# Strassen cross network: two 1024-row lanes that share each weight load, a second Strassen level in W22*T4, and two residual adds moved to DMA

## The chip, the cores and the metric

One core of a Trainium2 chip runs the kernel. The metric is the device time of one execution in microseconds (us), the median of several executions. Engines: PE is the matmul engine (PEld its weight load), DVE the vector engine, ACT the scalar engine, POOL is GpSimd, SP the engine that here only issues DMAs.

## The reference, cut to what matters

```python
B, Din, L = 16384, 1024, 6                  # bf16
def reference(x0, ws, bs):
    x = x0
    for l in range(L):
        proj = jnp.einsum('bd,de->be', x, ws[l]) + bs[l]
        x = x0 * proj + x
    return x
```

Rows are independent, so the kernel takes 1024 rows through all six layers and then takes the next 1024. x lives transposed (features on partitions), so x0 is transposed when it is loaded and the result is transposed again before it is stored. Both transposes are done by DMA.

## The kernel before: the parts that matter

Each layer is a 2x2 block product done with seven products in place of eight (Strassen, in Winograd's form). The product with W21 is itself done with seven half-size products, a second level. Weight combinations are built during the first pair of 512-row halves and saved to DRAM (`Lc`). Later pairs load eight 0.5 MB weight tiles per layer, up to eleven ahead.

```python
x0t_pool = ctx.enter_context(tc.tile_pool(name="x0t", bufs=2))   # x0 of this pair and of the next
xst_pool = ctx.enter_context(tc.tile_pool(name="xst", bufs=2))   # x of this pair and of the one before
wring    = ctx.enter_context(tc.tile_pool(name="wring", bufs=14))
PREF = 11
# ...
def tt(out, in0, in1, op):                                       # every DVE add, subtract, multiply
    nc.vector.tensor_tensor(out=out, in0=in0, in1=in1, op=op)
# ...
for pr in range(NPAIR):                     # 16 pairs of 512 + 512 rows
    for l in range(L):                      # 24 groups of four 128x512 matmuls
        # ...                               # and 7 small products of four 128x256 matmuls
        if l == (2 if pr == 0 else 0) and not last_pair:         # x0 of the NEXT pair, early
            x0T_next = x0t_pool.tile([P, 2, KD, NB], BF16, name="x0T")
            for n in range(2):
                tr = nc.sync.dma_start_transpose(out=x0T_next[:, n], in_=x0[...])
    # ... after the last layer: the result is transposed into the OLD x0 tile, then stored
    nc.sync.dma_start_transpose(out=xo, in_=xst[:].rearrange("r n k b -> r (n k b)"))
    for n in range(2):
        nc.sync.dma_start(out[...], x0T[:, n]...)
```

## Time and profile before

| | before |
|---|---|
| median | 2343.75 us (3 runs, 2342.72 to 2345.05) |
| PE, DVE, ACT busy | 97%, 86%, 78% |
| one layer of one pair, from the timeline | 23.78 us |
| 96 layers at 23.80 us | 2285 us |
| the rest of the profiled span of 2342.7 us: start, first pair's boundaries, end | 58 us |

Two lines of the page of the kernel before: busy us of each engine (share of the span) x instructions, and the shares of the chain of work that ended last.

```profile
PE 2277.5 (97%) x11668; PEld 1164.1 (50%) x11904; DVE 2003.2 (86%) x2160; ACT 1818.9 (78%) x2977; POOL 1.1 (0%) x5
...
PE 87%; DVE 10%; issue 1%; ACT 1%; SPq 1%; DMA 0%; DVEq 0%
```

PE sets the pace. What a matmul costs is read from the timeline, from start to start, because the second column (the duration) overlaps the next instruction. These are five lines of the timeline of the kernel before.

```profile
2276.54 1.03 PE L233 MATMUL pA_88<-xst,wp 128*128 128x512 bf16 x4
2277.41 1.03 PE L233 MATMUL pA_89<-xst,wp 128*128 128x512 bf16 x4
...
2286.90 0.60 PE L245 MATMUL pX_92<-xst,wp 128*128 128x256 bf16 x4
2287.34 0.60 PE L245 MATMUL pX_93<-ti,wp 128*128 128x256 bf16 x4
...
2300.32 1.03 PE L233 MATMUL pA_88<-xst,wp 128*128 128x512 bf16 x4
```

A group of four wide matmuls takes about 0.865 us, one of four narrow ones 0.44 us. From 2276.54 to 2300.32, one layer, it is 23.78 us.

The change from one pair to the next: these are the DMA queue of SP in the timeline, and the windows view of the same stretch (window and its length; busy us of PE, PEld, DVE, ACT, POOL; granted clock; DMA share of the 16 engines; GB/s), kernel before.

```profile
1191.49 9.73 SPq L374 DMA_TRANSPOSE x0T<-xst  x1
1201.32 0.52 SPq L83 DMA_DIRECT2D wp<-in_ws_dram  x1
...
1203.12 5.79 SPq L377 DMA_DIRECT2D out_dram<-x0T  x2
...
1215.50 10.67 SPq L355 DMA_TRANSPOSE x0T<-in_x_dram  x2
```

### The profile page before, as it was taken

What the parts mean: (1) busy time and instruction counts of PE and PEld (TensorE: products, weight loads), DVE (VectorE), ACT (ScalarE), POOL (GpSimd) and SP (SyncE); (2) the same over time, 40 slices, a digit from 0 to 9 for tenths busy, and PEclk for the clock granted to TensorE, in tenths of its full rate; (3) what the DMA queues carried; (4) which work ended last, traced back from release to release, by engine and by line L of the source; (5) the groups of instructions that cost most, each with busy time, mean ns of one, the idle gap of its engine ahead of it and who ended that gap; (6) DMA issues with size and microseconds to landing.
All of it is one profiled execution on the core that took longest, in us unless ns stands there. A gap on an engine that the chain in (4) does not pass through costs nothing.

```text
span 2342.7 us, 31963 instructions
## 1 busy us (share of the span) xinstructions
PE 2277.5 (97%) x11668; PEld 1164.1 (50%) x11904; DVE 2003.2 (86%) x2160; ACT 1818.9 (78%) x2977; POOL 1.1 (0%) x5
## 2 busy tenths in 40 slices
PE   6989999999999999999999999999999999999996
PEld 2445555555454555555555545454555555554543
DVE  5998888888889788888888888888898888988886
ACT  4767777878787787778787878778777777787775
POOL 0000000000000000000000000000000000000000
PEclk8999999999999999999999999999999999999998
DMA  7659669595785958759586695967859578595853
GB/s 242 198 198 239 229 193 267 182 257 198 206 256 185 274 187 213 252 178 284 174 222 240 189 276 171 254 206 207 253 189 271 193 204 257 175 284 178 234 191 81
DMA packets 613837, 508.60 MB, mean 217 GB/s; under 512 B 399664, under 2 KB 552240, under 8 KB 613680
## 3 DMA queue, kind: packets, MB, share of 16 engines
q1 hardware_dynamic: 613680, 506.53, 72.5%
q8 instruction: 95, 1.56, 0.3%
q14 instruction: 62, 0.51, 0.1%
HBM read 390.07 MB, written 49.28 MB: 188 GB/s over the span
## 4 chain that ended last, share of the span: by engine, by line
PE 87%; DVE 10%; issue 1%; ACT 1%; SPq 1%; DMA 0%; DVEq 0%
PE pA_91 L233 13%; PE pA_88 L233 13%; PE pA_89 L233 13%; PE pA_90 L233 12%; PE pX_92 L245 7%; PE pX_94 L233 6%; PE pX_93 L233 6%; PE pX_95 L233 6%; PE pX_92 L233 6%; DVE ev L91 4%; PE pX_93 L245 3%; DVE xst L91 2%; PE pX_94 L245 2%; DVE wp L91 1%; DVE ti L91 1%
## 5 line engine op out<-in xcount | busy, mean ns | idle before, releaser
L233 PEld LDWEIGHTS <-wp 128*128 128x128 bf16 x9216 | 901.4, 98 | 1026.5 <-issue 55.1
L91 DVE TENSOR_TENSOR ev<-ev,x0T 128x2048 bf16<-128x2048 bf16 x384 | 469.8, 1223 | 9.9
L91 DVE TENSOR_TENSOR xst<-ev,xst 128x2048 bf16<-128x2048 bf16 x320 | 384.9, 1224 | 21.7 <-DVE ev L91 0.5
L91 DVE TENSOR_TENSOR ev<-ev 128x2048 bf16<-128x2048 bf16 x288 | 352.2, 1223 | 38.0 <-ACT ev L249 25.7
L245 PEld LDWEIGHTS <-wp 128*128 128x128 bf16 x2688 | 262.7, 98 | 133.2
L252 ACT ACTIVATE ev<-pA_88,b_all 128x512 bf16<-128x512 f32 x288 | 198.4, 689 | 69.9 <-PE pA_88 L233 65.7
L252 ACT ACTIVATE ev<-pA_90,b_all 128x512 bf16<-128x512 f32 x288 | 198.1, 688 | 34.9 <-PE pA_90 L233 33.4
L252 ACT ACTIVATE ev<-pA_91,b_all 128x512 bf16<-128x512 f32 x288 | 197.9, 687 | 34.0 <-PE pA_91 L233 34.0
L252 ACT ACTIVATE ev<-pA_89,b_all 128x512 bf16<-128x512 f32 x288 | 198.3, 689 | 25.6 <-PE pA_89 L233 1.8
L245 PE MATMUL pX_92<-ti,wp 128*128 128x256 bf16 x1152 | 172.8, 273 | 1.1
L249 ACT CAST ev<-pX_92 128x512 bf16<-128x512 f32 x192 | 112.3, 585 | 28.8 <-PE pX_92 L233 16.7
L233 PE MATMUL pA_88<-xst,wp 128*128 128x512 bf16 x320 | 83.0, 382 | 22.4 <-DVE xst L91 22.4
L252 ACT ACTIVATE ev<-pX_92,b_all 128x512 bf16<-128x512 f32 x96 | 66.0, 687 | 26.6 <-PE pX_92 L233 24.3
L233 PE MATMUL pA_89<-xst,wp 128*128 128x512 bf16 x314 | 83.2, 385 | 0.3
L233 PE MATMUL pA_91<-xst,wp 128*128 128x512 bf16 x315 | 82.3, 381 | 0.6
L233 PE MATMUL pX_94<-xst,wp 128*128 128x512 bf16 x320 | 82.1, 379 | 0.3
L233 PE MATMUL pA_90<-xst,wp 128*128 128x512 bf16 x306 | 81.7, 385 | 0.4
L233 PE MATMUL pX_93<-xst,wp 128*128 128x512 bf16 x308 | 80.5, 379 | 0.7
L233 PE MATMUL pX_95<-xst,wp 128*128 128x512 bf16 x308 | 80.5, 379 | 0.3
L233 PE MATMUL pX_92<-xst,wp 128*128 128x512 bf16 x306 | 80.3, 379 | 0.4
L252 ACT ACTIVATE ev<-pX_93,b_all 128x512 bf16<-128x512 f32 x96 | 66.0, 687 | 16.9 <-PE pX_93 L233 15.7
L252 ACT ACTIVATE ev<-pX_94,b_all 128x512 bf16<-128x512 f32 x96 | 66.0, 687 | 16.9 <-PE pX_94 L233 16.9
(2831 smaller groups left out, 3586.4 us busy)
## 6 DMA issues: line engine op xcount, KB each, us to landing
wp<-Lc SPq DMA_DIRECT2D x450, 512.0 KB, 4.3
wp<-in_ws_dram SPq DMA_DIRECT2D x288, 512.0 KB, 4.9
out_dram<-x0T SPq DMA_DIRECT2D x30, 1024.0 KB, 10.2
Lc<-wp SPq DMA_DIRECT2D x30, 512.0 KB, 6.3
out_dram<-xoS SPq DMA_DIRECT2D x4, 512.0 KB, 4.7
w_98<-in_ws_dram SPq DMA_DIRECT2D x1, 512.0 KB, 5.0
x0T<-in_x_dram SPq DMA_TRANSPOSE x32, 7.3
w_151<-in_ws_dram SPq DMA_DIRECT2D x1, 512.0 KB, 5.4
```

The costliest lines, as they stand in the source:

```text
L91: nc.vector.tensor_tensor(out=out, in0=in0, in1=in1, op=op)
L233: nc.tensor.matmul(dst[m][:], lhsT=wt[:, k, m * P:(m + 1) * P], rhs=rhs[:, k, :], start=(start and k == 0), stop=(k == KH - 1), skip_group ...
L245: nc.tensor.matmul(dst[:, m * NQ:(m + 1) * NQ], lhsT=wv[:, k, m * P:(m + 1) * P], rhs=ti[i][:, k, :], start=(start and m == 0 and k == 0), ...
L249: nc.scalar.copy(out=dst, in_=src)
L252: nc.scalar.activation(out=dst, in_=src, func=IDENT, bias=bias_col(eh, m), scale=1.0)
```

## The change

The intent has three parts. (1) Two lanes of 1024 rows take turns layer by layer, so a weight tile is loaded once for both, and the dependent work of one lane (sums, differences, residual) runs under the matmuls of the other. (2) From the second lane pair on, the product W22*T4 also gets a second Strassen level: 20 groups and 14 small products per unit (one layer of one lane) instead of 24 and 7. (3) The residual adds of two of four quarters of x are done by an accumulating DMA from GpSimd's queue in layers 1 to 4. The memory for the second lane comes out of the double buffers.

The diff, cut to its core (helpers, first-pass weight combinations and the order of evictions left out):

```diff
-    x0t_pool = ctx.enter_context(tc.tile_pool(name="x0t", bufs=2))
-    xst_pool = ctx.enter_context(tc.tile_pool(name="xst", bufs=2))
-    wring = ctx.enter_context(tc.tile_pool(name="wring", bufs=14))
+    wring = ctx.enter_context(tc.tile_pool(name="wring", bufs=RING))        # RING = 10
+    x0L = [res.tile([P, 2, KD, NB], BF16, name=f"x0L{i}") for i in range(2)]   # one per lane
+    xL = [res.tile([P, 2, KD, NB], BF16, name=f"xL{i}") for i in range(2)]     # one per lane
# ...
+    def load_x0(lp, lane, eh, n):                      # a quarter, over the old x0, in place
+        r0 = lp * LB + lane * PR + n * NB
+        nc.sync.dma_start_transpose(out=q(x0L[lane], eh, n), in_=x0[r0:r0 + NB, eh * H:(eh + 1) * H])
+    def store_quarter(lp, lane, eh, n, xf):
+        # ...
+        nc.sync.dma_start_transpose(out=dst, in_=xf[:].rearrange("r j k p -> r (j k p)"))   # dst in xL
+        nc.sync.dma_start(out[r0:r0 + NB, eh * H:(eh + 1) * H]..., q(xL[lane], eh, n)...)
# ...
+    l2_of = lambda lp: (2,) if lp == 0 else (2, 4)     # products with a second level
+    units = [(lp, l, lane) for lp in range(NLP) for l in range(L) for lane in range(2)]
# ...
+        def x_out(c, eh, n):
+            if last_layer:
+                xf = late["xf"].tile([P, KH, KH, P], BF16, name="xf")          # pool of 2
+                tt(xf[:]..., c..., q(xst, eh, n)..., ADD)
+                store_quarter(lp, lane, eh, n, xf)
+            elif l > 0:
+                nc.gpsimd.dma_start(q(xst, eh, n), c, accum_op=ADD)
+            else:
+                tt(q(xst, eh, n), c, q(x0T, eh, n), ADD)
+        def finish(c, add, eh, n):
+            tt(c, c, add, ADD)
+            tt(c, c, q(x0T, eh, n), MULT)              # last use of this quarter of x0 ...
+            if nxt_x0:
+                load_x0(lp + 1, lane, eh, n)           # ... so it can be overwritten only now
+            x_out(c, eh, n)
```

A lane-pair switch, the term used below, is the passage from layer 5 of one lane pair to layer 0 of the next. There are seven, and each brings eight x0 loads and eight output transposes, every one a quarter of a lane (0.5 MB).

## The prediction

> What bounds the kernel now. The page gives PE 97% of 2342.7 us, DVE 86%, ACT 78%; the chain of waits is 87% PE, 10% DVE. In the timeline four 128x512 matmuls (one group) take 0.8645 us, four 128x256 ones 0.4365 us. One layer of a 1024-row pair is 24 groups plus 7 second-level products: 24 x 0.8645 + 7 x 0.4365 = 23.80 us, and the timeline shows 23.78 from layer to layer. 96 of these are 2285 us. The other 58 us are the start (first matmul at 11.8 us, then matmuls at half rate until 16.5), the first pair's layer boundaries where the new weights' combinations sit on DVE (the waits: PE for DVE's xst, 22.4 us in 5 times, each followed by slow matmuls), and 18 us after the last matmul.
>
> What the change does to PE. A layer of a lane becomes 20 groups plus 14 small products: 17.29 + 6.11 = 23.40 us, in 84 of 96 units (the first lane pair keeps 23.80). Sum 2251 us: 34 us less. All of it is critical.
>
> Boundaries. A lane's dependent work runs under the other lane, so the 22 us of boundary waits should go. The start gets worse: the second small product needs the combination of W21, W21 itself and the first differences; by the trace's durations PE stands until about 25 us (now 11.8). I put the start at 27 us lost, the tail at 19 as now. 2251 + 27 + 19 = 2297.
>
> DVE. A 128x512 add costs 0.42 us, a 128x2048 one 1.22; issued back to back 0.34 and 1.14. A wide 128x4096 one I estimate at 2.3. A middle layer then needs about 21.2 us of 23.4 (now 20.9 of 23.8); layers 0 and 5, without the DMA adds, about 23.6, thus just over PE. DVE goes to about 93% busy, with no slack in those layers. ACT drops a little: evictions of two banks at once.
>
> DMA. Weights are read 9 times 0.5 MB per two units instead of 16 times: queue share falls from 72% to about half. The new risk is the accumulating DMA. The Trainium skill (DMA: Bandwidth & Descriptors, Anatomy of one DMA) gives about 2 us fixed plus bytes/436 GB/s; with two reads per write, and traffic, my estimate is 6 to 9 us for 0.5 MB; no run here shows one yet. After the x12 product DVE does 8 us of other work before it needs the sum; the loop closes at landing time + 13.4 us per unit, so up to 10 us cost nothing, and each further us costs 1 us in 56 to 64 units. Descriptors come from GpSimd, beside a DVE always at two-input adds; SBUF — State Buffer (Who interferes with whom) says such adds take only the shared read port.
>
> Lane-pair switch. 16 quarter transposes at 2.4 us of SP issue each (DMA issues: 2.4 for xoS) plus stores that wait for them share the queue with weight loads only one ring ahead. I charge about 2 us of PE per switch, 15 us in all, and 6 us for small stalls.
>
> Predicted 2318 us, range 2283 to 2375. Chances: faster by over 2% 0.28, within 2% 0.57, slower 0.15.
>
> What would show it: middle layers at 23.4 us per lane in the timeline; no PE wait for DVE's xst in the first layers; PE first continuous at about 25 us; DVE over 90%; accumulating DMAs landing under 10 us; PE gaps, if any, at the switches, waiting for weights.
>
> What would make it wrong: accumulating DMAs over 10 us (then DVE stands before its first difference and PE follows: slower); the SP queue blocked in the switches for 8 us or more each (plus 60 us); or everything hidden (about 2290).

## More of the kernel before

```profile
1190.00:1200.00 10.00, 9.95 (x59) 5.67 (x58) 4.30 (x6) 7.72 (x14) 0.00 (x0) 1.00 0.99 211
1200.00:1210.00 10.00, 9.95 (x49) 4.73 (x49) 9.66 (x10) 8.46 (x14) 0.00 (x0) 1.00 1.08 266
1210.00:1220.00 10.00, 9.95 (x53) 5.12 (x53) 9.15 (x11) 7.82 (x14) 0.00 (x0) 1.00 1.06 219
```

For 30 us the DMA share is about 1, so the engines are busy all the time by this measure. (The share adds up the times of packets. It goes over 1, so packets overlap, and it does not tell how much room is left.) One output transpose and two x0 transposes keep SP for 20 us. PE nevertheless works 9.95 of each 10 us. Nothing that PE needs at that moment depends on those transfers.

## The result, and the profile after

The change made the kernel slower: 2417.51 us median (4 runs, 2416.68 to 2417.71) against 2344.4 us for the kernel before (4 runs). The ratio is 1.0311 (95% interval 1.0293 to 1.0329). Ratios here are the mean time of one kernel's runs over that of the other's of the same rounds, so not quite the ratio of the medians quoted. The time is above the predicted range, which ended at 2375.

The same two lines of the page, kernel after.

```profile
PE 2286.9 (95%) x12912; PEld 1269.5 (53%) x12912; DVE 2116.1 (88%) x2096; ACT 1783.9 (74%) x2485; POOL 110.7 (5%) x133
...
PE 77%; DVE 15%; DMA 5%; SPq 1%; issue 1%; ACT 1%; DVEq 0%; ACTq 0%
```

PE's share of the chain fell from 87% to 77%, and DMA appears with 5%. To see where, I took the time from one unit's first eviction on ACT to that of the next unit. This is worked out from the trace and is not a view of the profile. Rows are lane pairs; columns are the 12 units of one, layer by layer, lane 0 and lane 1.

```
before (two pairs per row)
2  23.8  23.8  23.8  23.8  23.8  23.8  23.8  23.8  23.8  23.8  23.8  23.8 | 285.3
after
0  33.5  23.8  24.0  23.8  23.8  23.8  23.8  23.8  23.8  23.8  23.8  23.8 | 295.3
1  35.9  24.9  24.1  23.4  23.4  23.4  23.4  23.4  23.4  23.4  23.4  23.4 | 295.3
2  37.5  25.0  24.1  23.4  23.4  23.4  23.4  23.4  23.4  23.4  23.4  23.4 | 297.0
...
6  38.6  24.3  24.1  23.4  23.4  23.4  23.4  23.4  23.4  23.4  23.4  23.4 | 297.5
```

Nearly everything went as counted. Middle units take 23.4 us, the first lane pair has no stalls between layers, and PE ends 18 us before the span does. Only the first unit or two of lane pairs 1 to 7 are long. Those seven rows sum to 2083.2 us, against 7 x 12 x 23.4 = 1965.6. The excess is 118 us, 17 us per switch, and without it the kernel would be at about 2299 us. By the trace, 86 us of the excess are gaps of PE (39 gaps of over 0.3 us), and about 32 us are matmuls at half clock after them (65 us of granted clock 0.5 in the switches).

What PE waits for, waits view of the kernel after (engine, line, waited for: us in total, times, longest):

```profile
PE XB L259 <- DMA wp<-Lc: 45.5, 12, 5.9
PE XB L259 <- DMA wp<-in_ws_dram: 18.3, 7, 7.8
PE XA L247 <- ACT P5s L239: 16.1, 13, 3.4
PE XA L247 <- DMA wp<-Lc: 11.9, 7, 3.1
```

Apart from one wait of 7.8 us at the start, these are late weights in the switches (68 us). ACT's eviction P5s waits in turn for DVE's D. So the weights are late, and this is SP's queue in one switch (timeline, kernel after; second column is the time SP spends issuing).

```profile
1183.03 2.54 SPq L155 DMA_TRANSPOSE xL<-xf  x1
1187.88 0.38 SPq L156 DMA_DIRECT2D out_dram<-xL  x1
1188.35 5.30 SPq L150 DMA_TRANSPOSE x0L<-in_x_dram  x2
1193.76 5.96 SPq L155 DMA_TRANSPOSE xL<-xf  x2
1199.81 0.54 SPq L156 DMA_DIRECT2D out_dram<-xL  x1
1200.44 0.46 SPq L100 DMA_DIRECT2D wp<-in_ws_dram  x1
...
1220.87 1.97 SPq L155 DMA_TRANSPOSE xL<-xf  x1
1222.93 1.38 SPq L100 DMA_DIRECT2D wp<-Lc  x2
```

And PE in the same stretch. The bracket holds the idle time before the instruction and what ended it.

```profile
1205.80 0.61 PE L259 MATMUL XB<-x0L,wp 128*128 128x256 bf16 x4 [2.03 <-DMA wp<-in_ws_dram]
1208.51 1.03 PE L259 MATMUL XB<-ti,wp 128*128 128x256 bf16 x4 [2.09 <-DMA wp<-Lc]
1209.33 1.91 PE L247 MATMUL pA<-x0L,wp 128*128 128x512 bf16 x4
1211.04 1.91 PE L247 MATMUL XA<-t,wp 128*128 128x512 bf16 x4
...
1227.44 0.61 PE L259 MATMUL XB<-ti,wp 128*128 128x256 bf16 x4 [4.19 <-DMA wp<-Lc]
```

The weight that was issued at 1200.44 lands at 1205.8, when PE has been waiting for 2 us. Each of these waits also costs a second time. From 1209.33 to 1211.04 a group takes 1.71 us, twice its usual 0.865. The Trainium skill (TensorE: Matmul & The Clock Gate, Part 1) says that PE runs at half clock after about 3.4 us of idling and needs about as long a busy spell to get back. This trace agrees on the half rate, which came here already after two waits of about 2 us each with a little work between. The full rate was back at 1214.44, some 6 us after work went on at 1208.51.

The windows view, kernel after, columns as before (the granted clock of 0.78 from 1210 to 1220 is the half rate seen above):

```profile
1190.00:1200.00 10.00, 10.00 (x62) 5.82 (x60) 3.31 (x4) 7.93 (x12) 0.00 (x0) 1.00 1.18 217
1200.00:1210.00 10.00, 5.88 (x30) 2.89 (x29) 9.86 (x10) 4.34 (x8) 0.00 (x0) 0.88 0.99 298
1210.00:1220.00 10.00, 10.00 (x45) 5.05 (x44) 8.33 (x10) 5.71 (x9) 0.00 (x0) 0.78 1.07 291
1220.00:1230.00 10.00, 5.81 (x30) 2.93 (x28) 4.61 (x5) 3.96 (x6) 0.00 (x0) 0.90 1.05 269
```

The DMA engines are as busy as in the switch of the kernel before, but here PE drops to 5.9 of 10 us. Per row of input the two kernels transpose the same number of bytes. The difference is what depends on those bytes, and when.

The accumulating DMAs, which I had feared, are harmless: middle units take 23.4 us (DMA issues of the page, kernel after; last column is median us from issue to landing):

```profile
xL<-Q POOLq DMA_DIRECT2D x64, 512.0 KB, 5.7
xL<-S POOLq DMA_DIRECT2D x64, 512.0 KB, 6.4
```

### The profile page after: what moved, and what is told of

It reads as the page before. It is cut to its first block, busy times and chain, and to the rows that moved or that the text cites. A ratio compares the mean times of both kernels' runs of the same rounds, so it can differ in the third digit from the quotient of the medians. Undisturbed runs are those within 1.5% of the kernel's fastest.

```text
span 2414.6 us, 32963 instructions
## 1 busy us (share of the span) xinstructions
PE 2286.9 (95%) x12912; PEld 1269.5 (53%) x12912; DVE 2116.1 (88%) x2096; ACT 1783.9 (74%) x2485; POOL 110.7 (5%) x133
## 4 chain that ended last, share of the span: by engine, by line
PE 77%; DVE 15%; DMA 5%; SPq 1%; issue 1%; ACT 1%; DVEq 0%; ACTq 0%
PE pA L247 35%; PE XA L247 23%; PE XB L259 19%; DVE t L63 4%; DVE D L63 3%; DVE ti L63 3%; DMA xL<-xf 3%; DMA x0L<-in_x_dram 2%; DVE S L63 2%; SPq L150 1%; DVE xf L63 1%; DVE xL L63 1%; DVE Q L63 1%; ACT P5s L239 1%; DMA wp<-in_ws_dram 0%
## 5 line engine op out<-in xcount | busy, mean ns | idle before, releaser
L247 PE MATMUL pA<-t,wp 128*128 128x512 bf16 x3104 | 780.2, 381 | 0.0
L239 ACT CAST F<-XB 128x1024 bf16<-128x1024 f32 x360 | 364.3, 1012 | 291.0 <-PE XB L259 284.4
L259 PE MATMUL XB<-ti,wp 128*128 128x256 bf16 x2880 | 436.9, 275 | 52.4 <-DMA wp<-Lc 45.5
L247 PE MATMUL XA<-t,wp 128*128 128x512 bf16 x1536 | 400.6, 385 | 2.4 <-DMA wp<-Lc 2.4
L247 PE MATMUL XA<-xL,wp 128*128 128x512 bf16 x1280 | 326.8, 379 | 2.3 <-ACT P5s L239 2.3
L247 PE MATMUL pA<-xL,wp 128*128 128x512 bf16 x1280 | 328.5, 379 | 0.0
L242 ACT ACTIVATE U3s<-pA,b_all 128x512 bf16<-128x512 f32 x384 | 264.4, 688 | 39.4 <-PE pA L247 19.0
L242 ACT ACTIVATE P1s<-pA,b_all 128x512 bf16<-128x512 f32 x384 | 266.0, 693 | 26.3 <-PE pA L247 18.5
L242 ACT ACTIVATE U2s<-pA,b_all 128x512 bf16<-128x512 f32 x384 | 266.1, 693 | 14.4 <-PE pA L247 5.1
L63 DVE TENSOR_TENSOR D<-D,x0L 128x4096 bf16<-128x4096 bf16 x96 | 220.0, 2292 | 13.3 <-ACT D L242 9.4
L63 DVE TENSOR_TENSOR t<-xL 128x4096 bf16<-128x4096 bf16 x80 | 183.4, 2293 | 23.4 <-DMA xL<-S 14.7
```

The costliest lines, as they stand in the source:

```text
L63: return nc.vector.tensor_tensor(out=out, in0=in0, in1=in1, op=op)
L239: nc.scalar.copy(out=dst, in_=src)
L242: nc.scalar.activation(out=dst, in_=src, func=IDENT, bias=bias_col(eh, m), scale=1.0)
L247: nc.tensor.matmul(dst, lhsT=w_[:, k, m * P:(m + 1) * P], rhs=b_[:, k, :], start=(start and k == 0), stop=(k == KH - 1), skip_group_check= ...
L259: nc.tensor.matmul(dst[:, m * NQ:(m + 1) * NQ], lhsT=wv[:, k, m * P:(m + 1) * P], rhs=b_[:, k, :], start=(start and m == 0 and k == 0), st ...
```

## The experiments

Fifteen kernels ran. "Excess" is, as above, the sum of the unit times of lane pairs 1 to 7 less 1965.6 us. It comes from the profiled run. Ratios are to the kernel before. In w_on_act the long unit is the last of a lane pair, so the first switch lies in row 0 and is added here (170 us without it). For pinned_light_ends, 28 of the 84 units count as 23.8 us, since it changes them.

| run | what it changes in the changed kernel | median us | ratio | excess us |
|---|---|---|---|---|
| (the change itself) | | 2417.5 | 1.031 | 118 |
| w_on_pool | weight loads from GpSimd's queue | 2515.1 | 1.072 | 216 |
| w_on_act | weight loads from ACT's queue | 2491.6 | 1.063 | about 190 |
| stores_on_pool | output stores from GpSimd's queue | 2452.1 | 1.047 | 152 |
| no_x0_reload (wrong result) | x0 loaded for the first lane pair only | 2315.1 | 0.987 | 17 |
| no_out_transpose (wrong result) | output stored untransposed | 2317.7 | 0.989 | 24 |
| xf_three | third buffer for the final sum | 2417.0 | 1.031 | 117 |
| swap_buffers | x0 and x swap buffers at a switch | 2426.4 | 1.035 | 130 |
| swap_and_defer | the same, 6 of 8 output transposes later | 2377.8 | 1.014 | 80 |
| defer_more | later still; W21 loaded second | 2389.9 | 1.020 | 87 |
| defer_more_ring11 | the same, 11 weight buffers | 2389.7 | 1.020 | 90 |
| no_dma_adds | residual adds back on DVE | 2492.1 | 1.064 | (DVE-bound) |
| one_second_level | no second level in W22*T4 | 2393.2 | 1.021 | 66 over 23.8 per unit |
| pinned | defer_more, output behind the x0 loads | 2314.7 | 0.987 | 13 |
| no_transposes (wrong result) | neither x0 reload nor output transpose | 2297.9 | 0.980 | 4 |
| pinned_light_ends | pinned, no second level on W22*T4 in layers 0 and 5 | 2308.1 | 0.985 | about 0 |

The theories. A: the weights wait on SP's queue behind slow issues and blocked stores. B: a switch holds more transfer work than its time allows, whatever the queue. D: DVE, which waits 95 us for one of the two buffers of the final sum, sets the pace.

### Another queue for the weights, or for the stores

```diff
-            st["dma"] = nc.sync.dma_start(t_[:], w_src(key[1], key[2]))
+            st["dma"] = nc.gpsimd.dma_start(t_[:], w_src(key[1], key[2]))    # w_on_act: nc.scalar
```

> Weight prefetches issued from GpSimd's queue in place of SP's; nothing else. Theory A (weights arrive late at a lane-pair switch because SP issues them in order behind 16 transposes of 2 to 6 us of issue each and behind stores that wait): PE's 76 us of waits for weights mostly go, the excess of a switch falls from about 17 us to 5 or less, total 2320 to 2340. Theory B (the 16 DMA engines are full in the switch, share 1.0 to 1.2 for 50 us, so weights are late on any queue): 2390 or more. Theory D (DVE waiting 95 us for a free xf buffer sets the pace): PE's wait only changes its name, 2380 or more.

> Weight prefetches issued from ACT's queue. Theory A: the same gain as from GpSimd's queue, 2320 to 2340, less ACT's issue time of 0.4 us for each of 9 loads per two units, which ACT's 26% idle hides. If only GpSimd's descriptors, not the other queue, helped, this one stays at 2400. Theory B: 2390 or more.

stores_on_pool makes the same edit to the store of `store_quarter`.

> Only the 64 output stores go to GpSimd's queue; transposes and weights stay on SP. In the switch at 1170 to 1245 us SP waited only 7 us for transposes to land before stores and spent about 6 us issuing stores; transposes' own issue was about 52 us. Theory A in the form 'issue time of transposes': small gain, 2375 to 2405. Theory A in the form 'head of line: stores that wait block the weights': 2350 or less. Theory B: no change.

All three were slower, not faster. stores_on_pool missed what every theory had forecast for it: 2452 us, with PE's waits for weights no shorter (80 us, before this edit 76). Why it was slower than the changed kernel was not followed up. In w_on_pool the weights do come in time inside the switches, and the transposes pay. SP's queue, timeline of w_on_pool:

```profile
1231.69 10.61 SPq L150 DMA_TRANSPOSE x0L<-in_x_dram  x2
1242.40 17.55 SPq L155 DMA_TRANSPOSE xL<-xf  x2
```

Two output transposes take 17.55 us of issue; in the kernel after, two took 5.96. Seven weight loads of GpSimd's queue landed while they were issued, and SP had no weights to issue, so SP's own list of work is not what slowed them. Over a whole switch SP spent 59 to 77 us on the 16 transposes, in the kernel after 45 to 52. The time moved to DVE's waits for the final sum's buffer (217 us, before this edit 95), to PE's waits for x0 and for DVE's differences. The Trainium skill (DMA: Bandwidth & Descriptors, Issuing engines are not separate DMA queues) says that DMAs of all issuing engines run on the same 16 engines and that several queues save only the time of issuing. This run agrees: what the weights gained on another queue the transposes lost, 2515 us in all. Theory A falls as the main cause. B's direction holds, though I had expected late weights of it and got late transposes.

w_on_act is not as clean. ACT itself stood still. Timeline of w_on_act:

```profile
1261.88 0.69 ACT L242 ACTIVATE U3s<-pA,b_all 128x512 bf16<-128x512 f32 x1 [17.83 <-DMA out_dram<-xL]
```

A weight load in ACT's stream had, by the profile, to wait for an earlier DMA (an output store), and the evictions behind it waited too. The same queueing problem had been moved to an engine that PE depends on.

### Taking half of the transposes away

```diff
 # no_x0_reload (wrong result)
-            if nxt_x0:
-                load_x0(lp + 1, lane, eh, n)        # and the two in tail_a
 # no_out_transpose (wrong result)
-        nc.sync.dma_start_transpose(out=dst, in_=xf[:].rearrange("r j k p -> r (j k p)"))
         nc.sync.dma_start(out[r0:r0 + NB, eh * H:(eh + 1) * H].rearrange("(j p) d -> p j d", p=P),
-                          q(xL[lane], eh, n).rearrange("p j d -> p j d"))
+                          xf[:].rearrange("r j k p -> r j (k p)"))
```

> Wrong result on purpose: x0 of the first lane pair is kept for all, so 56 of the 64 x0 transposes go, half of the switch's transposes. Theories A and B both expect most of the 118 us back: 2300 to 2330. Theory D (xf buffers, fed by the other transposes) expects at most half: 2360 or more, if the output transposes alone still take SP's queue as long.

> Wrong result on purpose: the last layer's sum is stored as it is, without the 64 transposes of the output; x0's transposes stay. After the runs with the weights on other queues (weights in time, but transposes landing in 15 to 18 us in place of 4.5, and slower in all), theory B is: a switch has 16 transposes, 8 stores and 14 weight loads for about 47 us of time, DMA engines over 100% busy, and the lane buffers force them there. B expects this run to get back most of the 118 us, like the one without the x0 reload: 2300 to 2330. Theory D2 (only the reload of x0 matters, because it overwrites x0 in place and comes late): 2370 or more.

Either half gives back about 100 us of 118: 2315 and 2318. (Without the output's transposes the end is 5 us shorter too, and this is counted in the 2318.) Neither kind alone is the cause of 100 us; it takes both together. That fits theory B, but these runs do not tell too much work from work in a bad order. Taking both away:

> Wrong result on purpose: neither x0's reload nor the output's transposes, the rest as in the changed kernel. If the switch costs by its transposes alone: no excess, 2296 to 2304 (2251 us of matmuls, 28 at the start, 18 at the end). If DVE's layers 5 and 0 alone cost PE time: 2310 or more.

It ran in 2297.9 us, with 4 us of excess. The rest of the changed kernel, the DVE-heavy layers 5 and 0 included, costs nothing in a switch on its own. The sum in the prediction before its allowance for switches and small stalls was 2297; that the two agree so closely is partly luck, because the end takes 13 us in this run and not 18.

### A third buffer for the final sum

```diff
-            late["xf"] = ctx.enter_context(tc.tile_pool(name="xfp", bufs=2))
+            late["xf"] = ctx.enter_context(tc.tile_pool(name="xfp", bufs=3))
```

> A third buffer for the final sum that waits for its transpose. Theory D (DVE's 95 us of waits for this buffer set the pace): 2350 or less. Theory B: the transposes take as long as before, so 2395 to 2415.

2417.0 us, no difference. DVE's waits in xf_three:

```profile
DVE t L63 <- DMA x0L<-in_x_dram: 69.7, 7, 10.6
...
DVE xf L63 <- DMA xL<-xf: 9.0, 7, 2.2
```

The 95 us of waiting for this buffer became 9, and the wait for x0 grew from 25 to 70. Theory D falls: a long wait in the list was only the first of several in a row.

### Giving the output time

The final sum can go into the quarter of x0 that has just died, and the next x0 into the dead quarter of x. The two resident buffers of a lane swap roles. Then the result may lie there for more than a unit, and its transposes can be issued later.

```diff
+    def final_add(c, xst, x0T, eh, n):                 # into the dead quarter of x0
+        v = q(x0T, eh, n)...
+        tt(v, c..., q(xst, eh, n)..., ADD)
+                    load_x0(lp + 1, lane, eh, n, xst)  # next x0 into the dead quarter of x
+        xo = late["xf"].tile([P, KH, NB], BF16, name="xo")                    # pool of 3
+        nc.sync.dma_start_transpose(out=xo[:]..., in_=q(src, eh, n)...)
+            x0L[lane], xL[lane] = xL[lane], x0L[lane]
 # swap_and_defer, in addition
+            if lane == 1 and last_layer and idx in (9, 12):
+                flush_one(0)                            # issue one waiting output quarter of lane 0
+            if lane == 0 and l == 0 and idx in (4, 7, 9, 12):
+                flush_one(1)
```

> At a switch the two resident buffers of a lane swap roles: the final sum goes into the dead quarter of x0, the next x0 is loaded into the dead quarter of x, and the output transposes have a pool of three tiles to land in. DVE no longer waits for a buffer; the order of the DMAs on SP stays, x0 first, then output. Theory D: 2350 or less. Theory B with order (weights and x0 still share the window with all 8 output transposes): 2370 to 2410.

> As the one before, and six of the eight output transposes of a switch are issued later: lane 0's last two after lane 1's first x0 load, lane 1's four in the next unit, behind all x0 loads and most weights. The same DMA work is spread over about one unit (23 us) more. Theory B (window too short for the work): most of the 118 us come back, 2305 to 2340, switch excess under 5 us. If the work itself and not its deadline is what costs: 2390 or more.

The swap alone gained nothing (2426.4, and B with order had said 2370 to 2410). Deferring six of eight output transposes gained 49 us over it (2377.8), so spreading the same work helps, but less than I had expected of theory B: 80 us of excess were left. The next step deferred more, and an eleventh weight buffer went beside it.

```diff
-            if lane == 1 and last_layer and idx in (9, 12):
+            if lane == 0 and l == 0 and idx in (2, 4):
                 flush_one(0)
-            if lane == 0 and l == 0 and idx in (4, 7, 9, 12):
+            if lane == 0 and l == 0 and idx in (7, 9, 12, 15):
                 flush_one(1)
+    prefetch()                                          # at the start: W21 before x0
     load_stage(0)
```

> All of a switch's late output transposes (lane 0's last two and lane 1's four) are issued in the first unit of the next lane pair, so that only weights and x0 loads and two output transposes are left in the tight window; and W21 is loaded second, ahead of x0, so that its combination is ready early. Theory B: switch excess 1 to 5 us (10 us in the run that deferred less), total 2300 to 2335 with about 7 us from the start. If the window is not what limits: 2370 as before.

> The same with an eleventh weight buffer (each load can be issued one weight earlier) and two landing tiles for output in place of three. Theory B: at most 5 us less per switch than the run beside it; if weight waits in the switch are already gone, no difference (within 10 us).

Both missed: 2390, slower than the run that deferred less, and the deeper ring changed nothing. (The early W21 gained nothing either. The first unit got 8 us shorter, but that run's first lane pair and start together were no shorter, because the wait came back in the next two units.) The waits of PE in defer_more tell what happened:

```profile
PE XA L267 <- ACT P5s L259: 37.7, 14, 4.5
PE XB L279 <- DMA xL<-in_x_dram: 16.4, 4, 5.1
...
PE XB L279 <- DMA x0L<-in_x_dram: 9.4, 4, 3.5
```

No weight is late any more; x0 is. DVE waits 89 us for it, and the evictions P5s wait for DVE. SP's queue in the same run shows why:

```profile
1205.50 9.31 SPq L157 DMA_TRANSPOSE xo<-xL  x2
1214.93 4.47 SPq L150 DMA_TRANSPOSE x0L<-in_x_dram  x2
```

Although the output comes later in the program, the scheduler that orders SP's stream had placed output transposes ahead of lane 1's last two x0 loads. Probably their data was ready first. So I forced the order, with an edge that costs no wait:

```diff
+        if lp + 1 < NLP:
+            tc.add_manual_dep(tr.ins, st["x0"].ins.name, NOSYNC, reason="output behind the x0 loads")
```

> As defer_more, with an order forced: each output transpose is issued after the last x0 load before it in program order. If the order of x0 and output transposes on SP is what cost 11 us in the second unit of a switch: that unit falls from 35 to 30 us or less, total 2335 to 2360. If DMA throughput in that stretch is the limit whatever the order: 2380 or more.

2314.7 us, correct, ratio 0.9873 (0.9859 to 0.9886). That is better than I had written down: the excess fell from 87 to 13 us with the same transposes, the same bytes and the same buffers. SP's queue in pinned now has the same two kinds in the other order:

```profile
1174.71 5.20 SPq L150 DMA_TRANSPOSE x0L<-in_x_dram  x2
1179.96 4.66 SPq L157 DMA_TRANSPOSE xo<-xL  x2
```

The waits of PE in pinned:

```profile
PE XA L269 <- ACT P5s L261: 13.7, 16, 4.8
PE pA L269 <- DMA x0L<-in_x_dram: 12.4, 1, 12.4
...
PE XB L281 <- DMA wp<-Lc: 1.2, 1, 1.2
```

The 12.4 us are the first load of the program. So B needs one more word: the switch holds too much transfer work ahead of its deadlines. The work itself did not shrink. In pinned the 16 transposes of a switch take 50 to 55 us of SP and 67 to 73 us from first issue to last landing; in the changed kernel they take 45 to 52 and 67 to 71 (both from the trace). Moving what has no near deadline out of the way was enough. The pinned kernel also contains the swap, the deferral and the early W21; the forced order alone, in the changed kernel, was not run.

### The other two parts of the change

```diff
 # no_dma_adds
-                nc.gpsimd.dma_start(q(xst, eh, n), c, accum_op=ADD)
+                tt(q(xst, eh, n), c, q(xst, eh, n), ADD)
 # one_second_level
-    l2_of = lambda lp: (2,) if lp == 0 else (2, 4)
+    l2_of = lambda lp: (2,)
```

> Only the residual adds of x11 and x12 go back from accumulating DMAs to DVE. Prediction's count: 2 x 1.2 us more on DVE in each of 64 middle units, 21.2 to 23.6 us against PE's 23.4. If DVE's count is right, the middle units turn DVE-bound and lengthen by 0.1 to 0.5 us, total 2415 to 2450; if the DMA adds had a cost of their own (landing too late, contention), the run is faster than 2410.

2492.1 us. The middle units went from 23.4 to about 24.25 us, DVE-bound. The direction was as counted, the size was not. DVE is busy 193.7 us in the 200 us from 400 to 600, which is 23.5 us per unit and close to the 23.6 that I had put; but it did not reach 100% busy, and the unit takes 24.25. The accumulating DMAs are the part of the change that lets the rest fit, and they save about 75 us.

> Only the second Strassen level in W22*T4 is undone: 24 groups and 7 small products in all units, 23.80 us in place of 23.40. Expected 84 x 0.4 = 34 us more in the middle units; DVE has about 2.5 us less per unit, so a switch may cost a few us less: 2430 to 2450. If the small products cost more than their matmuls (waits for evictions), the loss is smaller than 34 us.

2393.2 us: faster by 24, where I had expected a loss. Middle units are 23.8 us, as counted, which costs 34 us. The excess of the switches, though, went from 118 to 66 us, probably because DVE has less to do behind the late x0 (148.0 us busy in the 200 us from 400 to 600, in the changed kernel 183.0); this run does not show that by itself. With the switch repaired, it can be tested on purpose:

> As pinned, and the second level in W22*T4 left out in layers 0 and 5 only: 28 units are 0.4 us longer on PE (11 us in all), and DVE has about 3 us less to do in each. If DVE's chain behind the late x0 is part of the remaining excess, the excess falls by more than 1.6 us per switch beyond that and the total is at or below pinned; if only transposes count, it is 11 us above pinned.

2308.1 us (2306.4 to 2308.5), correct, ratio 0.9846 (0.9832 to 0.9859), and no excess is left. (Of the 9.4 us between the two profiled runs, 4.5 lie in lane pairs 1 to 7 and 2.7 at the end, which is shorter as well.) This is the fastest correct version here, 1.5% faster than the kernel before and 4.5% faster than the changed one (2308.1 over 2417.5, from medians of different rounds).

## Why the prediction was wrong

Point by point:

- Units at 23.40 us in place of 23.80: right, 23.4 in the unit table. 2251 us of matmuls stand.
- Layer boundaries of the first pair go, the start loses 27 us, the end 19: right. Summing row 0 and the time to its first eviction gives 28 us lost at the start, and the end takes 18.
- DVE at 21.2 us per middle unit: right as busy time (183.0 us busy in the 200 us from 400 to 600, which is 21.4 per 23.4). That DVE can be filled up to 100% was wrong: in no_dma_adds a unit takes 24.25 with 23.5 busy. DVE's total share was 88%, not 93: its 2116 us would be 91% of the predicted 2318, and the span grew.
- Accumulating DMAs under 10 us: right. They landed in 5.7 and 6.4 us; the estimate was 6 to 9. That DVE's two-input adds do not hold up their descriptors, which the skill's page (SBUF — State Buffer, Who interferes with whom) led me to expect, agrees with these landings; no run isolates it.
- The switch: wrong, and this is the step that failed. "I charge about 2 us of PE per switch, 15 us in all". It cost 17 us per switch, 118 in all. That is 103 us more than charged, and the miss is 99.5 (2417.5 against 2318); the 6 us for small stalls did not come.

The mechanism was named, for weights and transposes on one queue, and even listed under what would make the prediction wrong ("8 us or more each"). What the sentence did not name is x0 itself: in defer_more no weight is late, and 87 us are lost to late x0. The term was mis-sized for two reasons. First, I added up SP's issue times alone, at the 2.4 us that a transpose takes in quiet, 38 us for 16. In the switches of the changed kernel they took 45 to 52 us of SP, and 67 to 71 us from the first issue to the last landing. This alone is not the loss, because the transposes of pinned take as long. Second, I did not ask what the lost double buffers had been good for. In the kernel before, the same transposes keep the DMA engines as busy while PE loses nothing, because x0 is loaded a pair ahead and the result may leave a pair later. The change keeps one tile per lane for each. x0 can then only be loaded between its last use in layer 5 and its first use in layer 0, and the result must leave in that same gap.

What is shown: the excess lies in the switches, needs both kinds of transposes, and nearly vanishes when the output yields to x0 and weights. Still open is what limits the transposes of a switch, SP's issuing or the DMA engines; no run measured one by itself, and none issued transposes from another queue.

## What to carry to other kernels

When a change pays for its gain with a double buffer, look up which transfers that buffer had kept free of deadlines, and count all the work that now must land between the last use and the next use, from the first issue to the last landing rather than by issue times in quiet. Busy DMA engines cost nothing here where what came late was what nobody waited for, so order transfers by their deadlines before moving them to other queues. Check the order that was really issued in the trace.

## What the Trainium skill lacked or had wrong

- DMA: Bandwidth & Descriptors, DMA Transpose (X-bar): no page gives the time that a transpose of this size holds its queue beside other traffic; this page has sequencer cycles for "previous generations" (small tiles, or 8,192 tiles) and an effective bandwidth. A 512x512 bf16 quarter took 2.4 us of SP's time in quiet (median, kernel before) and landed after 4.6; in w_on_pool single ones took up to 20.6 us of issue and landed after up to 36.5.
- The same page, on issuing from several engines: it says this "will only save the time on the sequencer". Here it did harm: 2515 and 2492 us against 2417.5, with weights on GpSimd's and on ACT's queue.
- The same page gives about 2 us plus bytes over 436 GB/s for a DMA from GpSimd, which is an estimate of 3.2 us for 0.5 MB. Accumulating in SBUF beside other traffic it was 5.7 and 6.4 us. No page has a figure for an accumulating DMA within one core.
- TensorE: Matmul & The Clock Gate gives an idle window of about 3.4 us before PE falls to half clock. Here two waits of 2.0 and 2.1 us with four small matmuls between them were enough (1.71 us per group after 1209.33).
